# A kernel of Nystrom attention and an MLP: the order of VectorE's work for the coming set of batches, written anew

## The chip, the cores and the metric

The kernel runs on one core of a Trainium2 chip. Its time is the device time of one execution in microseconds (us). Lower is better. Each engine of the core (TensorE, VectorE, ScalarE, GpSimd) works through its own instructions in order, and SyncE issues the DMAs; in the profile they are PE, DVE, ACT, POOL and SP.

## The reference

Eight batches of eight heads, 576 positions, 64 dimensions a head. Softmax attention is approximated over 32 landmarks (means over 18 neighbouring positions), with an iterated pseudo-inverse in between; the result is laid out as 4608 rows of 512 and goes through a layer norm and an MLP with a hidden width of 2048, whose output is added to it.

```python
q_lm = q.reshape(B, H, m, S // m, D).mean(axis=3)      # m = 32 landmarks
k_lm = k.reshape(B, H, m, S // m, D).mean(axis=3)
A, Bm, C = sm(q, k_lm), sm(q_lm, k_lm), sm(q_lm, k)    # sm: softmax of the scaled product
Z = Bm.T / (norm_1(Bm) * norm_inf(Bm) + 1e-06)
for _ in range(6):
    Z = 2 * Z - Z @ Bm @ Z
x = A @ Z @ C @ v                                      # then heads side by side: [8, 576, 512]
xn = (x - mean(x)) / sqrt(var(x) + 1e-06) * g_ln
out = x + maximum(xn @ w_ch1, 0) @ w_ch2
```

## The kernel before

The attention of the batches and the MLP run interleaved on TensorE. Batches 0 and 1 are treated one at a time (`attention`); the others in four **sets**, (2), (3, 4), (5, 6) and (7) (`attention2`). A batch has two **units** of four heads each.

**The MLP stream.** `mlp()` is a generator over nine groups of 512 rows (four **blocks** of 128). Each step gives one matmul: for a group 64 of psh (hidden layer, sixteen tiles of four), with ACT's Relu to hT after each tile, and 64 of pso (output, four tiles of sixteen), with VectorE's ot (scale and add x) after each tile and the store on SP. `fill(n)` takes n steps of it; it returns early when the stream has nothing that it may do. Group 1's input is turned by TensorE (`transposes(1)`: four psxt tiles of four matmuls, each copied to xnT by ACT): during group 0's pso if block 7 is normalized by then, which `ln_ready` tells, and otherwise in a row ahead of group 1's psh. From group 2 on a DMA transpose on SP does it, issued after GpSimd's xn.

**The attention of a set.** `attention2` yields after each of its steps: for each pair of units the scores of k (psb, and psec with ACT's exp ec and VectorE's turn ecT); then the product with v (pscv, gathered for one pair a step) after the gram matrix (psse); six iterations (psn on TensorE, st on VectorE), the first ones with the scores of q for a pair of units (psea, ACT's exp ea); zc (pszc, zcbd); then the **rows**, in pieces of up to 128: two matmuls psy, and on VectorE rcpd and xblk. When a block's rows are complete `block_done` sets off its mean, centering and squares (negm, xn, junk), some of it deferred to `settle` and `a_square`. A set of one batch has 14 steps, a set of two has 21.

**The coming set.** While one set is in its attention the next is prepared (class `Coming`). For each tile of q or k: a load on SP, a cast to fp16 on GpSimd (nat), and on VectorE a **turn** (a transpose, xT<-nat). Each k also has a **sum** over its segments on VectorE (`add_up`: two TENSOR_REDUCE into part); so have the q of the first units, as many as `first_by_pool` says; for the other q GpSimd adds (asum, s) and VectorE turns the result (sT) and adds two halves into part. For each pair of units a **spread** on TensorE (psl<-part) makes the landmarks, copied to lm, from which psb and psec read. These turns, sums and spreads are the **jobs**, in a fixed order; `prepare(c, casts, jobs)` issues so many casts and jobs. Before, one job is issued at every step, and what is left goes into a loop ahead of the set's scores.

**Order.** All engines keep the order in which the program issues (`keep`), stores aside. A matmul that waits for VectorE holds all matmuls behind it. PSUM has three pools: ps1 (one buffer), ps2 (two buffers, taken in turn by psec, pscv, psea, pszc and psy) and psM (three buffers, for psh, pso, psxt and psl).

Batch 1's own attention (generator `a1`) is drained before the sets; its rows come in five pieces, the first one the second half of block 4, the others blocks 5 to 8. Block 7 is the last of group 1.

Of the kernel before, what the change touches and what calls it, by code (L numbers as in the profile page):

```python
# [9 lines left out]
FP16 = mybir.dt.float16  # L10
# [6 lines left out]
P = 128  # L17
# [3 lines left out]
def kernel(  # L21
# [12 lines left out]
    B, H, S, D = q.shape  # L34
# [4 lines left out]
    LM = 32  # L39
# [12 lines left out]
        name=nc.get_next_instruction_name(), act_func_set_id=6, ins=[], outs=[]))  # L52
# [16 lines left out]
    dve, pool, scalar = Ordered(nc.vector), Ordered(nc.gpsimd), Ordered(nc.scalar)  # L69
    act = scalar.activation  # L70

    def MM(o, l, r, rb=0, cb=0, start=True, stop=True, skip=False):
        keep(nc.tensor.matmul(o, l, r, start=start, stop=stop, tile_position=(rb, cb),  # L73
                              skip_group_check=(skip or cb != 0)))
# [88 lines left out]
    for half in range(2):  # L163
        for e in range(2):
            sl = ds(64 * e + 32 * half, 32)
            nc.gpsimd.tensor_copy(
                out=spread16[sl, half, e, :, :],
                in_=ident16[sl, sl][:, None, :].broadcast_to([LM, 2, LM]))
# [23 lines left out]
    for u in range(U):  # L192
        for nm in ("q", "k"):
            cast_qk(0, u, nm, dve)
        if u == 0:

            dve.tensor_copy(out=bones[:], in_=mask4[:, :, None].broadcast_to([P, 4, 32]))
            for i, t in enumerate(zcbd_buf):
                dve.tensor_copy(out=t[:, ds(0 if i % 2 == 0 else 4 * D, 4)],
                                in_=(mask4[:] if i < 2 else heads_of[i % 2]))  # L200
# [43 lines left out]
    asm = ctx.enter_context(tc.tile_pool(name="asm", bufs=2))  # L244
# [263 lines left out]
    class Coming:  # L508
# [38 lines left out]
        def cast(self, i):  # L547
            nm, w = self.parts[i]
            b, u = self.units[w]
            stg = self.stg.pop(i)  # L550
            if nm == "v":
                natv_of[b] = natv_buf[b % NV]
                pool.tensor_copy(
                    out=natv_of[b][:, u, :, :, 0:D].rearrange("p j r d -> p r j d"), in_=stg[:])
                return
            t = nat.tile([P, 2, NJ, D], FP16, name="nat", tag="nat")
            pool.tensor_copy(out=t[:], in_=stg[:])
            self.n16[i] = t
            if nm == "q" and w >= self.first_by_pool:
                s = asum.tile([P, 2, 4, D], FP32, name="asum", tag="asum")  # L560
                s16 = asm.tile([P, 2, D], FP16, name="s16", tag="s16")
                self.sums[i] = s16
                for o, x, y in ((s[:], t[:, :, 0:4, :], t[:, :, 4:8, :]),
                                (s[:, :, 0:2, :], s[:, :, 0:2, :], s[:, :, 2:4, :]),
                                (s[:, :, 0, :], s[:, :, 0, :], s[:, :, 1, :]),
                                (s16[:], s[:, :, 0, :], t[:, :, 8, :])):
                    with nc.allow_low_precision("sums are rounded once, to fp16"):
                        pool.tensor_tensor(out=o, in0=x, in1=y, op=ALU.add)
# [6 lines left out]
        def turn(self, i):  # L575
            nm, w = self.parts[i]
            t = aprep.tile([P, 2, NJ, LM, 2], FP16, name="xT", tag="xT" + nm, bufs=5 if nm == "q" else 4)
            dve.transpose(t[:].rearrange("p r j t x -> p (r j t x)").bitcast(UINT32),
                          self.n16.pop(i)[:].rearrange("p r j d -> p (r j d)").bitcast(UINT32))
            self.xT[nm, w] = t  # L580
            if i in self.sums:
                s = asm.tile([P, 2, LM // 2, 2, 2], FP16, name="sT", tag="sT")
                dve.transpose(s[:].rearrange("p r l a x -> p (r l a x)").bitcast(UINT32),
                              self.sums.pop(i)[:].rearrange("p r d -> p (r d)").bitcast(UINT32))
                dve.tensor_tensor(out=self.part_of(nm, w), in0=s[:, :, :, 0, :], in1=s[:, :, :, 1, :],
                                  op=ALU.add)
# [12 lines left out]
        def spread(self, y):  # L599
            part = self.part.pop(y)  # L600
            psl = psM.tile([P, 2, 8, LM], FP32, name="psl", tag="pm")
            for half in range(2):
                MM(psl[:, half, :, :].rearrange("p k c -> p (k c)"),
                   spread16[:, half, :, :, :].rearrange("p e a w -> p (e a w)"),
                   part[:].rearrange("p n w r l x -> p (n w r l x)"))
            lm = asm.tile([P, 8, 2, LM], FP16, name="lm", tag="lm", bufs=3)
            dve.tensor_copy(out=lm[:].rearrange("p k h c -> p h k c"), in_=psl[:])
            for i, nm in enumerate(("q", "k")):
                for x in range(2):
                    self.lm[nm, 2 * y + x] = lm[:, ds(4 * i + 2 * x, 2), :, :].rearrange(  # L610
                        "p r h (l x) -> p r (h l) x", x=2)
# [126 lines left out]
    def settle():  # L738
        while later:
            later.pop(0)()  # L740
# [156 lines left out]
    def fill(n):  # L897
        for _ in range(n):
            if not next(stream, False):
                return  # L900
# [49 lines left out]
    a1 = attention(1)  # L950
# [6 lines left out]
    cast_v(1)  # L957
    fetch_w2()

    sets = [Coming((2,), 1), Coming((3, 4), 2), Coming((5, 6)), Coming((7,))]  # L960

    def prepare(c, casts, jobs):
        for _ in range(casts):
            if c.casts:
                c.next_cast()
                if not c.loads and c is not sets[-1]:
                    sets[sets.index(c) + 1].next_load()
                else:
                    c.next_load()
        for _ in range(jobs):  # L970
            c.next_job()
# [6 lines left out]
    def a_square():  # L978
        if squares:
            squares.pop(0)()  # L980

    n = 0
    for what in a1:
        fill(fills[what])
        settle()
        if what in ("iteration", "product"):
            a_square()
        if what in ("product", "zc", "rows"):
            n += 1
            prepare(sets[0], 1, 1 if n > 3 else 0)  # L990
    for _ in range(2):
        prepare(sets[0], 1, 1)
        fill(6)

    counts = [[9, 20] + 6 * [6] + [7] + 4 * [7] + [10]]
    counts += [[8, 12, 18, 18, 10, 10, 8, 8, 8, 8, 8] + 10 * [7]]
    counts += [[12, 14, 20, 20, 12, 12, 12, 10, 10, 10, 10] + 10 * [10]]
    counts += [[15, 18] + 6 * [12] + [12] + 5 * [12]]
    for c, after, count in zip(sets, sets[1:] + [None], counts):
        while c.jobs:  # L1000
            prepare(c, 1, 1)
            fill(3)
        for step, _ in enumerate(attention2(c.bs, c)):
            fill(count[step])
            settle()
            if step >= 2:
                a_square()
            if after:
                prepare(after, 1, 1)
    for _ in stream:  # L1010
        pass

# [29 lines left out]
```

## Time and profile before

| | us |
|---|---|
| median of 3 runs | 330.3 (329.87 to 331.22) |
| the profiled execution | 330.62 |
| its span, first to last instruction | 328.9 |
| TensorE busy | 312.6 |
| VectorE busy | 152.3 |
| ScalarE busy | 150.9 |
| GpSimd busy | 121.2 |

The span is shown in forty slices of 8.2 us each, with the busy share in tenths, and the clock that TensorE was granted in tenths of full speed. A row of a timeline has the start, the duration, the engine, line and operation, output and inputs, the shape, how many, and in brackets the idle time ahead and what ended it. A row of a table by groups ends with busy us and the mean in ns, then the idle time ahead. All operations pass through one helper, so they have the same line; their tiles tell them apart.

### The profile page before, as it was taken

What the parts mean: (1) busy time and instruction counts of PE and PEld (TensorE: products, weight loads), DVE (VectorE), ACT (ScalarE), POOL (GpSimd) and SP (SyncE); (2) the same over time, 40 slices, a digit from 0 to 9 for tenths busy, and PEclk for the clock granted to TensorE, in tenths of its full rate; (3) what the DMA queues carried; (4) which work ended last, traced back from release to release, by engine and by line L of the source; (5) the groups of instructions that cost most, each with busy time, mean ns of one, the idle gap of its engine ahead of it and who ended that gap; (6) DMA issues with size and microseconds to landing.
All of it is one profiled execution on the core that took longest, in us unless ns stands there. A gap on an engine that the chain in (4) does not pass through costs nothing.

```text
span 328.9 us, 7899 instructions
## 1 busy us (share of the span) xinstructions
PE 312.6 (95%) x3248; PEld 157.1 (48%) x3248; DVE 152.3 (46%) x398; ACT 150.9 (46%) x295; POOL 121.2 (37%) x186
## 2 busy tenths in 40 slices
PE   8879999599989999989999999999999999999994
PEld 7557654244434444444544444444444444444443
DVE  3677259767987556955464345431243120010012
ACT  3476843339533670469413574563048207305600
POOL 4489877863799290449700020500010300000000
PEclk9999999699999999999999999999999999999999
DMA  7999999948998695871023112320241124032023
GB/s 283 391 387 386 386 389 256 371 125 218 283 272 270 201 258 176 250 140 33 2 66 72 29 32 64 83 48 2 64 103 28 32 64 96 2 75 53 2 56 72
DMA packets 38700, 50.32 MB, mean 153 GB/s; under 512 B 17540, under 2 KB 17800, under 8 KB 38664
## 3 DMA queue, kind: packets, MB, share of 16 engines
q1 hardware_dynamic: 38664, 49.82, 52.7%
q8 instruction: 25, 0.41, 0.6%
q14 instruction: 11, 0.09, 0.1%
HBM read 36.70 MB, written 9.44 MB: 140 GB/s over the span
## 4 chain that ended last, share of the span: by engine, by line
PE 81%; DVE 13%; DMA 3%; issue 1%; SPq 0%; ACT 0%; DVEq 0%
PE psh L73 39%; PE pso L73 31%; DVE xblk L67 3%; DVE part L67 3%; DMA stg<-in_k_dram 2%; PE psn L73 2%; PE psy L73 2%; DVE xT L67 2%; PE pscv L73 2%; DVE ot L67 1%; PE psec L73 1%; DMA xnT<-xn 1%; DVE rcpd L67 1%; PE psea L73 1%; DVE rcv L67 1%
## 5 line engine op out<-in xcount | busy, mean ns | idle before, releaser
L73 PE MATMUL psh<-xnT,w 128*128 128x512 f16 (+1 forms) x640 | 135.1, 358 | 1.2 <-DMA xnT<-xn 1.2
L73 PE MATMUL pso<-w,hT 128*128 128x512 f16 (+1 forms) x592 | 135.0, 377 | 0.6 <-issue 0.6
L67 ACT ACTIVATE hT<-psh 128x512 f16<-128x512 f32 x144 | 84.7, 598 | 89.2 <-PE psh L73 88.9
L73 PEld LDWEIGHTS <-w 128*128 128x128 f16 x640 | 59.1, 98 | 58.9 <-issue 2.9
L73 PEld LDWEIGHTS <-hT 128*128 128x128 f16 x592 | 56.6, 99 | 60.5 <-issue 4.2
L67 DVE SCALAR_TENSOR_TENSOR ot<-pso,rstd,xblk 128x512 f32<-128x512 f32 (+1 forms) x37 | 27.2, 734 | 76.6 <-PE pso L73 76.3
L67 POOL TENSOR_SCALAR negm<-rowsum 128x1 f32<-128x1 f32 x28 | 5.3, 190 | 97.9 <-DVE xblk L67 94.4
L67 ACT ACTIVATE junk<-xblk,negm 128x512 f16<-128x512 f32 x36 | 26.0, 721 | 24.9 <-POOL negm L67 24.8
L67 POOL CAST nat<-stg 128x1152 f16<-128x1152 f32 x28 | 31.8, 1145 | 14.4 <-DMA stg<-in_q_dram 9.4
L67 DVE SCALAR_TENSOR_TENSOR xblk<-psy,rcpd 128x512 f32<-128x512 f32 (+1 forms) x40 | 27.6, 691 | 2.2
L67 DVE SCALAR_TENSOR_TENSOR st<-st,psn 128x128 f16<-128x128 f16 (+2 forms) x36 | 11.4, 316 | 33.3 <-PE psn L73 33.2
L67 POOL CAST natv<-stg 128x1152 f16<-128x1152 f32 x16 | 18.4, 1162 | 7.3 <-DMA stg<-in_v_dram 7.3
L67 DVE TENSOR_REDUCE part<-xT 128x32 f16<-128x576 f16 x30 | 21.0, 743 | 0.0
L67 POOL TENSOR_SCALAR xn<-xblk,negm 128x512 f16<-128x512 f32 x28 | 19.2, 692 | 4.1 <-DMA xnT<-xn 3.1
L67 DVE RECIPROCAL rcpd<-psy 128x8 f32<-128x8 f32 (+1 forms) x40 | 8.1, 202 | 23.9 <-PE psy L73 23.8
L67 DVE STREAM_TRANSPOSE xT<-nat 128x576 uint32<-128x576 uint32 x24 | 18.4, 765 | 0.0
L73 PE MATMUL psy<-zcbd,ea 128*128 128x260 f16 (+1 forms) x80 | 15.7, 276 | 0.9 <-DVE zcbd L67 0.8
L73 PEld LDWEIGHTS <-st 32*32 32x32 f16 x448 | 5.7, 89 | 15.9 <-issue 10.6
L73 PEld LDWEIGHTS <-ea 128*128 128x128 f16 (+1 forms) x80 | 7.3, 100 | 10.5 <-issue 2.2
L67 ACT ACTIVATE ea<-psea 128x576 f16<-128x576 f32 x12 | 7.2, 648 | 10.7 <-PE psea L73 10.7
L67 ACT ACTIVATE ec<-psec 128x576 f16<-128x576 f32 x12 | 8.9, 814 | 6.8 <-PE psec L73 6.8
L67 POOL TENSOR_TENSOR asum<-asum 128x256 f32<-128x256 f32 (+1 forms) x18 | 10.7, 592 | 1.4
(101 smaller groups left out, 209.9 us busy)
## 6 DMA issues: line engine op xcount, KB each, us to landing
stg<-in_q_dram SPq DMA_DIRECT2D x16, 576.0 KB, 7.3
stg<-in_k_dram SPq DMA_DIRECT2D x16, 576.0 KB, 9.0
out_dram<-ot SPq DMA_DIRECT2D x70, 128.0 KB, 2.3
wstg<-in_moe_w_ch_dram SPq DMA_DIRECT2D x16, 512.0 KB, 6.9
stg<-in_v_dram SPq DMA_DIRECT2D x10, 576.0 KB, 7.3
stg<-in_v_dram SPq DMA_DIRECT2D x12, 288.0 KB, 9.2
xnT<-xn SPq DMA_TRANSPOSE x28, 2.5
out_dram<-ot SPq DMA_DIRECT2D x4, 64.0 KB, 2.0
```

What stands on the lines that cost most here:

```text
L67: return lambda *args, **kw: keep(getattr(self.engine, op)(*args, **kw))
L73: keep(nc.tensor.matmul(o, l, r, start=start, stop=stop, tile_position=(rb, cb), skip_group_check=(skip or cb != 0)))
```

## The change

The fill counts and jobs of every step are written out as pairs (count, jobs). For batch 2 both q sums go to GpSimd, for set (3, 4) all but the first. The loop over `a1` ends after the third of its five pieces of rows; the last two follow batch 2's first two steps, each behind that step's matmuls. Set (3, 4) is prepared by one job in eight of batch 2's steps, set (5, 6) by one job in the last seven of the steps of (3, 4), set (7) from the second step of (5, 6) on. The loop ahead of a set's scores gives five matmuls a job and not three. A cast of q or k isn't issued while eight tiles wait for their turn. ACT copies psl to lm, and no longer VectorE. The tiles s16 and sT have four and one buffers, two each before.

```diff
--- before.py
+++ after.py
@@ -558,7 +558,7 @@
             self.n16[i] = t
             if nm == "q" and w >= self.first_by_pool:
                 s = asum.tile([P, 2, 4, D], FP32, name="asum", tag="asum")
-                s16 = asm.tile([P, 2, D], FP16, name="s16", tag="s16")
+                s16 = asm.tile([P, 2, D], FP16, name="s16", tag="s16", bufs=4)
                 self.sums[i] = s16
                 for o, x, y in ((s[:], t[:, :, 0:4, :], t[:, :, 4:8, :]),
                                 (s[:, :, 0:2, :], s[:, :, 0:2, :], s[:, :, 2:4, :]),
@@ -579,7 +579,7 @@
                           self.n16.pop(i)[:].rearrange("p r j d -> p (r j d)").bitcast(UINT32))
             self.xT[nm, w] = t
             if i in self.sums:
-                s = asm.tile([P, 2, LM // 2, 2, 2], FP16, name="sT", tag="sT")
+                s = asm.tile([P, 2, LM // 2, 2, 2], FP16, name="sT", tag="sT", bufs=1)
                 dve.transpose(s[:].rearrange("p r l a x -> p (r l a x)").bitcast(UINT32),
                               self.sums.pop(i)[:].rearrange("p r d -> p (r d)").bitcast(UINT32))
                 dve.tensor_tensor(out=self.part_of(nm, w), in0=s[:, :, :, 0, :], in1=s[:, :, :, 1, :],
@@ -604,7 +604,7 @@
                    spread16[:, half, :, :, :].rearrange("p e a w -> p (e a w)"),
                    part[:].rearrange("p n w r l x -> p (n w r l x)"))
             lm = asm.tile([P, 8, 2, LM], FP16, name="lm", tag="lm", bufs=3)
-            dve.tensor_copy(out=lm[:].rearrange("p k h c -> p h k c"), in_=psl[:])
+            scalar.copy(lm[:].rearrange("p k h c -> p h k c"), psl[:])
             for i, nm in enumerate(("q", "k")):
                 for x in range(2):
                     self.lm[nm, 2 * y + x] = lm[:, ds(4 * i + 2 * x, 2), :, :].rearrange(
@@ -957,11 +957,11 @@
     cast_v(1)
     fetch_w2()
 
-    sets = [Coming((2,), 1), Coming((3, 4), 2), Coming((5, 6)), Coming((7,))]
+    sets = [Coming((2,)), Coming((3, 4), 1), Coming((5, 6)), Coming((7,))]
 
     def prepare(c, casts, jobs):
         for _ in range(casts):
-            if c.casts:
+            if c.casts and (c.parts[c.casts[0]][0] == "v" or len(c.n16) < 8):
                 c.next_cast()
                 if not c.loads and c is not sets[-1]:
                     sets[sets.index(c) + 1].next_load()
@@ -987,26 +987,29 @@
             a_square()
         if what in ("product", "zc", "rows"):
             n += 1
-            prepare(sets[0], 1, 1 if n > 3 else 0)
+            prepare(sets[0], 1, {4: 1, 5: 1, 6: 2}.get(n, 0))
+        if n == 6:
+            break
     for _ in range(2):
         prepare(sets[0], 1, 1)
-        fill(6)
-
-    counts = [[9, 20] + 6 * [6] + [7] + 4 * [7] + [10]]
-    counts += [[8, 12, 18, 18, 10, 10, 8, 8, 8, 8, 8] + 10 * [7]]
-    counts += [[12, 14, 20, 20, 12, 12, 12, 10, 10, 10, 10] + 10 * [10]]
-    counts += [[15, 18] + 6 * [12] + [12] + 5 * [12]]
-    for c, after, count in zip(sets, sets[1:] + [None], counts):
+        fill(8)
+
+    steps = [[(10, 0), (12, 1)] + 6 * [(7, 1)] + [(9, 1)] + 5 * [(6, 0)]]
+    steps += [[(6, 0), (8, 0), (10, 0), (8, 0), (4, 0), (4, 0), (4, 0), (5, 0), (5, 0), (5, 0), (8, 0)]
+              + 3 * [(6, 0)] + 7 * [(7, 1)]]
+    steps += [[(12, 0), (14, 1), (20, 1), (20, 1)] + 6 * [(11, 1)] + [(10, 1)] + 10 * [(10, 1)]]
+    steps += [[(15, 0), (18, 0)] + 6 * [(12, 0)] + [(12, 0)] + 5 * [(12, 0)]]
+    for c, after, plan in zip(sets, sets[1:] + [None], steps):
         while c.jobs:
             prepare(c, 1, 1)
-            fill(3)
-        for step, _ in enumerate(attention2(c.bs, c)):
-            fill(count[step])
+            fill(5)
+        for (count, jobs), _ in zip(plan, attention2(c.bs, c)):
+            fill(count)
             settle()
-            if step >= 2:
-                a_square()
+            a_square()
             if after:
-                prepare(after, 1, 1)
+                prepare(after, 1, jobs)
+            next(a1, None)
     for _ in stream:
         pass
```

## The prediction

> **What bounds the kernel now.** I read first the page's busy shares and slices, then TensorE's timeline for its gaps, then VectorE's timeline at the largest gap, then the table by stretches, last the prices by form. TensorE is busy 95% of the span; from 143 us on it shows no gap. So a change of order can win or lose only by TensorE's gaps before that, and by its clock.
>
> ```profile
> PE 312.6 (95%) x3248; PEld 157.1 (48%) x3248; DVE 152.3 (46%) x398; ACT 150.9 (46%) x295; POOL 121.2 (37%) x186
> PE   8879999599989999989999999999999999999994
> PEclk9999999699999999999999999999999999999999
> ```
>
> The gaps that concern the change, from TensorE's timelines (start, duration; in brackets the idle time ahead and what ended it):
>
> ```profile
> 61.08 0.59 PE L73 MATMUL psl<-part,spread 128*128 128x256 f16 x2 [3.59 <-DVE part L67]
> 96.22 0.39 PE L73 MATMUL psl<-part,spread 128*128 128x256 f16 x2 [1.39 <-DVE part L67]
> ...
> 130.17 0.60 PE L73 MATMUL psy<-zcbd,ea 128*64 128x260 f16 x2 [0.26 <-DVE zcbd L67]
> 136.58 0.38 PE L73 MATMUL psl<-part,spread 128*128 128x256 f16 x2 [0.72 <-DVE part L67]
> 142.91 0.60 PE L73 MATMUL psh<-xnT,w 128*128 128x512 f16 x2 [1.19 <-DMA xnT<-xn]
> ```
>
> Three times a spread (psl) waits for part, the last of VectorE's turns and sums for the next set. VectorE's timeline before the first:
>
> ```profile
> 57.11 0.75 DVE L67 SCALAR_TENSOR_TENSOR ot<-pso,rstd,xblk 128x512 f32<-128x512 f32 x1
> 57.78 0.77 DVE L67 STREAM_TRANSPOSE xT<-nat 128x576 uint32<-128x576 uint32 x1
> 58.58 1.41 DVE L67 TENSOR_REDUCE part<-xT 128x32 f16<-128x576 f16 x2
> 59.91 0.77 DVE L67 STREAM_TRANSPOSE xT<-nat 128x576 uint32<-128x576 uint32 x1
> 60.60 0.20 DVE L67 STREAM_TRANSPOSE sT<-s 128x64 uint32<-128x64 uint32 x1
> 60.84 0.19 DVE L67 TENSOR_TENSOR part<-sT 128x64 f16<-128x64 f16 x1
> ```
>
> It has no idle time there: it is a queue of work that is longer than TensorE's cover. From start to start a turn takes 0.69 us, a sum (two TENSOR_REDUCE) 1.33, an ot 0.67, sT with part 0.46; one piece of rows (rcpd and xblk) 0.85. The stretches around it show what the gap costs beyond itself:
>
> ```profile
> core 0: us, PE busy (x) PEld busy (x) DVE busy (x) ACT busy (x) POOL busy (x), PEclk, DMA share, GB/s
> 53.40:60.20 6.80, 4.10 (x26) 2.04 (x25) 6.66 (x15) 3.16 (x6) 6.08 (x9) 1.00 1.05 333
> 60.20:67.00 6.80, 5.92 (x63) 2.49 (x63) 4.62 (x12) 2.17 (x4) 5.26 (x5) 0.50 1.00 343
> ```
>
> After the 3.59 us of idling the clock is halved for 6.8 us: 5.92 busy us at half speed lose about 3.0.
>
> [...] 3.59 us idle and 0.50 after it; gaps of 1.39 and less left it at 1.00. [...] the spread above waits out the ot and turns ahead of its part. [...] the row hT has 598 ns.
>
> ```profile
> L67 DVE CAST lm<-psl 128x512 f16<-128x512 f32 x6 | 4.1, 684 | 1.0 <-PE psl L73 1.0
> L67 ACT ACTIVATE hT<-psh 128x512 f16<-128x512 f32 x144 | 84.7, 598 | 89.2 <-PE psh L73 88.9
> L67 ACT ACTIVATE ea<-psea 128x576 f16<-128x576 f32 x12 | 7.2, 648 | 10.7 <-PE psea L73 10.7
> L67 ACT COPY xnT<-psxt 128x512 f16<-128x512 f16 x5 | 2.9, 579 | 3.1 <-PE psxt L77 3.1
> ```
>
> **The change, part by part.** An MLP matmul of 512 columns is 0.216 us, a psy pair 0.22.
>
> (1) Two q sums go to GpSimd: VectorE loses 2 x 1.33 and gains 2 x 0.46, GpSimd gains 2 x 2.77 (asum rows 1.156 + 0.730 + 0.455, s 0.426). Six lm copies of 0.684 leave VectorE, and cost ACT about 0.60 each. None ends a wait by itself; they enter below.
>
> (2) Batch 2's spread (61 us before). The third piece of rows starts at 50.02 as before. Then TensorE has 6 + 8 + 8 = 22 pso: ready at 50.24 + 4.75 = 55.0. VectorE's sum of k0 ends, with the third piece, at 53.25 as in the trace; then turn 0.69, sum 1.33, turn 0.69, sT and part 0.46, ot 0.67, turn 0.69, sT and part 0.46: 58.2. GpSimd's second s: the q cast at 48.85, sums from 50.0, cast of q1 from 53.0, sums to 57.1, so it is not last. Idle 3.26 us instead of 3.59: -0.3. The spread is 2.8 us earlier, but two psy pairs, two transposes' groups and six pso no longer lie ahead of it, so the cover has shrunk with the queue. I leave the half clock as it is (the gap is just shorter than before: bounds -3.0 to 0). lm from ACT is ready under five pso: -0.35 (that part of the wait ahead of psb).
>
> (3) The two moved pieces. Block 7 closes group 1 of the MLP, so its four transposes can't be woven into group 0's pso any more: the order has all 16 psxt matmuls in a row behind psea, and psh of group 1 behind them. Block 8's psy takes the PSUM buffer that the second psea tile needs. On VectorE, between the end of the last pso and that buffer's release, stand ot 0.67, the turn of the next set's k0 0.69, and the piece 0.85, with 0.2 of latency 2.4 us; TensorE has psy and psn, 0.35: a new gap of **2.05**. Then ACT has two ea (1.19 in the timeline) and four xnT copies (4 x 0.56) before psh may start: 3.4 us, against 16 transposes of 55 ns, 0.9: a second gap of **2.6**, with latencies. Sum +4.7. [...] I take no second half clock (bounds 0 to +3.4, as 5 us in 6 are idle). GpSimd's negm and xn of block 8 (0.19, 0.69) wait for that xblk, and the casts of the next set's q behind them; their turns come four iterations later, so nothing. Block 8's DMA transpose on SP moves along, needed a group (128 matmuls) later: nothing. Casts and loads stay one for each call of prepare, so SP's loads keep their places to within a few.
>
> (4) Set (3, 4): seven jobs are left for the loop ahead of its scores, with 5 matmuls each. From the last psy to the first spread TensorE has 0.22 + 21 x 0.216 = 4.76; VectorE starts 0.43 after psy (as at 145 us): 0.43 + 0.85 + sum 1.33 + ot 0.66 + turn 0.69 + sum 1.33 = 5.3. Gap 0.6, where 1.39 stood: -0.8.
>
> (5) Set (3, 4)'s own attention has 67 matmuls up to zc, 116 before. Six pso (1.3) under two ec (0.74 each on ACT), four psh (0.86) under two ea: +0.6 for these waits (bounds 0 to 2; the iterations' 0.95 from psn over st to psn is just covered by 1.06).
>
> (6) Set (5, 6)'s jobs now begin at the fourth of ten row pieces, seven matmuls a step, and the rest follow in the loop. From psy 4 to the first spread TensorE has 64 matmuls and 7 psy pairs, 15.4 us. VectorE, from 1.3 us after psy 4: four turns 2.8, four sums 5.3, two turns with sT and part 2.3, six pieces 5.1, four ot 2.6, in all 18.1: 19.4 us. Gap **4.05**, where 0.26 + 0.72 + 1.19 = 2.2 stood (the DMA wait of 142.9 goes, since block 15's rows come 60 matmuls ahead of their group): +1.9. It is longer than 3.59, so a half clock follows: +3.0 (bounds 0 to 3.4).
>
> Sum: -0.3 - 0.35 + 4.7 - 0.8 + 0.6 + 1.9 + 3.0 = +8.75. The profiled execution took 330.6 (span 328.9 and 1.7 around it), so 339.4; the median of three is 0.3 lower: **339.0**.
>
> **Rivals.** (a) The reordering works as VectorE's relief: 1.75 + 4.1 us leave it, the three waits for part and their half clock go, 3.6 + 3.0 + 1.4 + 0.7 + 1.2 = 9.9 less a gap of 2 to 3 at psea: 323. For it: these are the named waits. Against: the work ahead of each spread is shortened, but the matmuls ahead of it too; it decides from where VectorE's queue in (6) is under 15.4 us, 4 less than my sum. (b) The gaps are as summed but more clock is lost: [...] +3.4, and (5) costs its upper bound: 344. For it: 1.4 us of work in 6. [...] (c) Gaps as summed and no half clock at all, with that of 61 us gone too: 339.0 - 6.0 = 333. [...] (d) A wash, 330: only if (3) is hidden, and I see nothing that hides it.
>
> **How the numbers follow.** Half a per cent, 1.6 us, is about what a measurement of this kernel can tell from no change. Forecast 0.64; (b) 0.14; (c) 0.10; (d) 0.04; (a) 0.08. So slower 0.88, same 0.04, faster 0.08. The forecast alone spans 335.5 to 342; the range reaches to (c) and (b): 333 to 345.
>
> **What would show it.** Right: psl of batch 2 near 58.3 with about 3.3 us idle; the second psea tile released by xblk and psh of group 1 by ACT's xnT, two gaps of 2 to 3 us before 78; one gap of about 4 us ahead of set (5, 6)'s first psl and PEclk 0.5 after it; no wait for DMA xnT near it. Wrong: TensorE without a gap over 1 us between psea and psh, or the spread of (5, 6) released by something other than part, or VectorE's queue there idle.

## The result, and the profile after

The changed kernel takes **336.07 us** (median of 4 runs, 334.69 to 336.54), the kernel before 330.61 (4 runs, 329.87 to 331.22). The ratio is 1.016, with a 95% interval of 1.012 to 1.020: slower, by some 5.5 us. The profiled execution of the changed kernel took 336.52 us with a span of 334.8, against 330.62 and 328.9: 5.9 us more to explain. One of the runs reported below, 335.85 us of e1_rows_back, was in a slower state of the chip and is left out.

From the page of the changed kernel, the busy shares and the clock in forty slices (8.4 us each):

```profile
PE 314.9 (94%) x3248; PEld 156.9 (47%) x3248; DVE 147.7 (44%) x392; ACT 155.3 (46%) x301; POOL 126.8 (38%) x194
PEclk9999999787999999999999999999999999999999
```

VectorE did lose 4.6 us of work (152.3 before), ACT gained 4.4 and GpSimd 5.6, as the change says. TensorE's matmuls are the same in number; it is busy 2.3 us longer, most of it by the clock (slices 8 to 10: 10.2 us at half clock in all, 6.8 before), and the rest is gaps. These are its gaps over 0.4 us between 45 and 165 us, from TensorE's timeline of the changed kernel (start, duration, operation; in brackets the idle time ahead and what ended it):

```profile
58.72 0.38 PE L73 MATMUL psl<-part,spread 128*128 128x256 f16 x2 [4.16 <-DVE part L67]
70.01 0.50 PE L73 MATMUL psea<-xT,lm 32*32 32x288 f16 x28 [1.84 <-DVE xblk L67]
72.32 0.38 PE L77 MATMUL psxt<-ident,xn 128*128 128x128 f16 x4 [1.03 <-ACT xnT L67]
73.79 1.44 PE L73 MATMUL psh<-xnT,w 128*128 128x512 f16 x3 [1.09 <-ACT xnT L67]
104.36 0.39 PE L73 MATMUL psl<-part,spread 128*128 128x256 f16 x2 [1.37 <-DVE part L67]
148.16 0.38 PE L73 MATMUL psl<-part,spread 128*128 128x256 f16 x2 [0.47 <-ACT hT L67]
153.87 0.39 PE L73 MATMUL psl<-part,spread 128*128 128x256 f16 x2 [1.90 <-DVE part L67]
```

The reader is to see three things. The first spread still waits for VectorE, longer than before (4.16, not 3.59). Three new gaps, 3.96 us together, stand between 68 and 74 us, where the kernel before had none. And the spreads of the later sets wait 3.74 us in all, 2.11 before, and elsewhere; the wait of 1.19 us for DMA xnT is gone.

The table by stretches of the changed kernel, at the two places where the clock was halved. The second line shown is the stretch just ahead of the second fall:

```profile
core 0: us, PE busy (x) PEld busy (x) DVE busy (x) ACT busy (x) POOL busy (x), PEclk, DMA share, GB/s
59.41:62.83 3.42, 3.42 (x55) 1.19 (x54) 0.86 (x4) 1.31 (x4) 2.51 (x3) 0.50 1.04 371
...
69.65:73.06 3.41, 1.66 (x44) 1.18 (x45) 1.83 (x5) 2.46 (x5) 2.90 (x4) 1.00 0.89 247
73.07:79.89 6.82, 6.10 (x29) 1.83 (x29) 2.04 (x5) 4.21 (x11) 6.42 (x9) 0.50 1.06 219
```

Behind the first gap the half clock is shorter than before (3.4 us, not 6.8); a new one of 6.8 us follows the three new gaps.

To put a number on each stretch, I added up TensorE's lost time: for every matmul the time to the start of the next, less that time as its form has it when undisturbed (the fastest tenth of its form, in whichever of the two traces it is shorter). Gaps and half clock both count in it.

| stretch (its start before and after, us) | lost before | lost after | difference | the prediction's terms |
|---|---|---|---|---|
| start to batch 1's third piece of rows | 16.37 | 15.77 | -0.60 | 0 |
| from there (50.02, 49.42) to group 1's first psh | 8.09 | 12.49 | +4.40 | -0.3 - 0.35 + 4.7 = +4.05 |
| from there (69.94, 73.79) to group 2's first psh | 6.99 | 8.50 | +1.52 | -0.8 + 0.6 = -0.2 |
| from there (106.68, 111.99) to group 3's first pso | 8.83 | 9.27 | +0.44 | +1.9 + 3.0 = +4.9 |
| from there (160.53, 166.29) to the end | 7.94 | 8.08 | +0.15 | 0 |

They add up to the 5.9. The second stretch holds most of the change's price: losses of over 0.6 us at one place go from 3.75 to 8.90 there (the first spread +0.58, the three new gaps 4.57), all smaller ones from 4.34 to 3.59. The second half clock lies in the third stretch and costs 3.3 us there (73.79 to 79.89 us), so the rest of that stretch lost 1.8 us less than before.

### The profile page after: what moved, and what is told of

It reads as the page before. It is cut to its first block, busy times and chain, and to the rows that moved or that the text cites. A ratio compares the mean times of both kernels' runs of the same rounds, so it can differ in the third digit from the quotient of the medians.

```text
span 334.8 us, 7911 instructions
## 1 busy us (share of the span) xinstructions
PE 314.9 (94%) x3248; PEld 156.9 (47%) x3248; DVE 147.7 (44%) x392; ACT 155.3 (46%) x301; POOL 126.8 (38%) x194
## 4 chain that ended last, share of the span: by engine, by line
PE 73%; DMA 9%; DVE 7%; POOL 7%; issue 2%; ACT 1%; SPq 1%; POOLq 0%; DVEq 0%
PE psh L73 33%; PE pso L73 31%; DMA wstg<-in_moe_w_ch_dram 5%; POOL w L67 4%; DMA stg<-in_v_dram 2%; DMA stg<-in_q_dram 2%; DVE part L67 2%; PE psy L73 2%; DVE xT L67 2%; POOL asum L67 1%; DVE ot L67 1%; PE psn L73 1%; PE pscv L73 1%; PE psec L73 1%; DVE xblk L67 1%
## 5 line engine op out<-in xcount | busy, mean ns | idle before, releaser
L73 PE MATMUL psh<-xnT,w 128*128 128x512 f16 (+1 forms) x640 | 138.6, 363 | 1.1 <-ACT xnT L67 1.1
L73 PE MATMUL pso<-w,hT 128*128 128x512 f16 (+1 forms) x592 | 133.1, 376 | 0.0
L67 DVE TENSOR_REDUCE part<-xT 128x32 f16<-128x576 f16 x26 | 18.3, 745 | 0.1
L67 POOL TENSOR_TENSOR asum<-asum 128x256 f32<-128x256 f32 (+1 forms) x22 | 13.0, 593 | 1.7
L67 POOL TENSOR_TENSOR asum<-nat 128x512 f32<-128x512 f16 x11 | 12.7, 1155 | 0.9
```

Of the source, the lines that this page charges most:

```text
L67: return lambda *args, **kw: keep(getattr(self.engine, op)(*args, **kw))
```

## The experiments

My theory: the price is the two moved pieces of rows, some 4 us, and what the edits for VectorE save is small because a spread that comes earlier has less work ahead of it. The rivals: the new counts and jobs of set (3, 4) cost it, or the q sums and copies on GpSimd and ACT do. Later runs ask what would have helped. The table has medians, and ratios to the kernel before on the same chip. Four chips were used (e1 to e4, e5 to e8, e9 to e11, e12); the kernel before took 330.04 to 330.63 us on them.

| run | what it is | us | ratio (95%) |
|---|---|---|---|
| e1_rows_back | changed kernel, rows not moved | 331.83 | 1.0025 (1.0006 to 1.0044) |
| e2_rows_moved | before, rows moved | 334.19 | 1.010 (1.007 to 1.013) |
| e3_old_plan | changed kernel, set (3, 4) with the counts and jobs of before | 340.16 | 1.026 (1.019 to 1.033) |
| e4_relief | before, lm copies on ACT, q sums on GpSimd | 330.02 | 0.996 (0.994 to 0.999) |
| e5_cover | before, 18 more matmuls ahead of the first spread | 336.17 | 1.017 (1.013 to 1.021) |
| e6_cover_cut | e5, 28 fewer matmuls in set (3, 4) | 327.99 | 0.992 (0.989 to 0.996) |
| e7_relief_cover | e4 with cover and cut | 329.36 | 0.996 (0.994 to 0.998) |
| e8_piece_late | changed kernel, block 8's piece a step later | 338.12 | 1.026 (1.022 to 1.029) |
| e9_one_piece | changed kernel, only block 8's piece moved | 334.32 | 1.013 (1.009 to 1.017) |
| e10_best | e6, lm copies on ACT, cover moved | 325.98 | 0.988 (0.985 to 0.990) |
| e11_best_qsum | e10, one q sum more on GpSimd | 322.40 | 0.976 (0.973 to 0.979) |
| e12_tiles_only | e10 with e11's tiles alone | 325.10 | 0.985 (0.979 to 0.990) |

### The rows put back: e1_rows_back

```diff
-        if n == 6:
-            break
...
-            next(a1, None)
```

> The changed kernel, with all five row pieces of batch 1 ahead of the sets again (nothing moved behind batch 2's scores); all else as changed. Theory 1, the move costs the time (two gaps at psea and psh of group 1, and the half clock after them): 329 to 332, no gap between psea and psh, the transposes woven into group 0's pso. Rival, the plan by steps costs it (late jobs, few matmuls in set (3, 4)): 334 to 336. The first spread still waits some 3 us in both.

Measured: 331.83 us (329.85 to 333.42), 4.2 below the changed kernel. None of the gaps at psea and group 1's psh is left. From TensorE's timeline of this run:

```profile
60.95 0.38 PE L73 MATMUL psl<-part,spread 128*128 128x256 f16 x2 [1.34 <-ACT xnT L67]
```

The first spread waits 1.34 us here, and not for part: the two pieces are its cover again. (A psxt at 57.7 us waits 1.16 us, too, for ACT's xnT. At 119 us a psh waited 2.67 us, ended by nothing that the trace shows; other runs have a shorter stall near there or none.) So the move is worth 4.2 of the 5.5 us. Which of the other edits cost the rest, 1.2 us over the kernel before, no run here shows.

### The rows moved alone: e2_rows_moved

```diff
             prepare(sets[0], 1, 1 if n > 3 else 0)
+        if n == 6:
+            break
...
                 prepare(after, 1, 1)
+            next(a1, None)
```

> The kernel before, with the move of the last two row pieces alone (loop over batch 1's attention left after the third piece, one further piece after each of the first two steps). Theory 1: 335 to 338, all 16 transposes behind psea, gaps of about 1.8 and 2.1 us there, half clock after them. Rival (plan): 330 to 332.

Measured: 334.19 us (332.91 to 336.2), a little under what was expected, 3.6 above the kernel before. From its TensorE timeline:

```profile
70.98 0.73 PE L73 MATMUL psea<-xT,lm 32*32 32x288 f16 x28 [2.50 <-DVE xblk L67]
...
74.99 1.01 PE L73 MATMUL psh<-xnT,w 128*128 128x512 f16 x2 [0.89 <-ACT xnT L67]
```

The same two waits with the same releasers come with this edit alone. Moved from either side, the pieces cost 3.6 to 4.2 us: that is shown.

### Set (3, 4) counted as before: e3_old_plan

```diff
-    steps += [[(6, 0), (8, 0), (10, 0), (8, 0), (4, 0), (4, 0), (4, 0), (5, 0), (5, 0), (5, 0), (8, 0)]
-              + 3 * [(6, 0)] + 7 * [(7, 1)]]
+    steps += [[(n, 1) for n in [8, 12, 18, 18, 10, 10, 8, 8, 8, 8, 8] + 10 * [7]]]
```

> The changed kernel, with the counts and the one job a step of before for set (3, 4) alone. Theory 1: 334 to 337, as the gaps at psea and psh stay; the last spread of set (5, 6) then waits under 1 us instead of 1.9. Rival (plan): 330 to 332.

The edit also puts back one job at every step of this set. A miss: 340.16 us (339.24 to 340.7), 4.1 above the changed kernel, where 334 to 337 was expected; the last spread of set (5, 6) has no gap, as expected. One line of its TensorE timeline says why:

```profile
150.09 3.17 PE L73 MATMUL psh<-xnT,w 128*128 128x512 f16 x7 [4.32 <-DMA xnT<-xn]
```

With the old counts the MLP stream is so far ahead that it meets group 3 before block 15's DMA transpose has landed, and the clock is halved with it (148.4 to 155.3 us). So the new counts and jobs of this set are no part of the price; together they save about 4 us in the changed kernel. That rival falls.

### The relief alone: e4_relief

```diff
-            dve.tensor_copy(out=lm[:].rearrange("p k h c -> p h k c"), in_=psl[:])
+            scalar.copy(lm[:].rearrange("p k h c -> p h k c"), psl[:])
...
-    sets = [Coming((2,), 1), Coming((3, 4), 2), Coming((5, 6)), Coming((7,))]
+    sets = [Coming((2,)), Coming((3, 4), 1), Coming((5, 6)), Coming((7,))]
```

with the tiles s16 and sT as in the change.

> The kernel before, with the copies of psl by ACT and the two q sums on GpSimd alone. Relief of VectorE with nothing moved: the first spread waits 0.9 us less, the second 0.5 less: 328.5 to 330. Rival, that a longer GpSimd queue delays the sums or slows VectorE's small operations: 330 to 332.

Measured: 330.02 us (327.74 to 331.36), 0.6 below the kernel before. VectorE's work falls, yet the first spread waits 4.61 us there instead of 3.59, and set (3, 4)'s second one 2.10 instead of 1.39. There are two causes. With a job fewer in the queue, the spread is issued a pass of the loop, and so six matmuls, earlier, and TensorE comes to it 1.1 us earlier. And VectorE ends its queue hardly earlier, since its small additions took longer beside GpSimd's casts. From the whole timeline:

```profile
57.37 2.26 POOL L67 CAST natv<-stg 128x1152 f16<-128x1152 f32 x2
...
58.88 0.79 DVE L67 TENSOR_TENSOR part<-sT 128x64 f16<-128x64 f16 x1
...
60.98 0.39 PE L73 MATMUL psl<-part,spread 128*128 128x256 f16 x2 [4.61 <-DVE part L67]
```

This part took 0.79 us and the next one (60.52 us) 0.41, where the kernel before has 0.19 (60.84 us): 0.82 us of the 0.87 that the moved sum saves. That is the rival that the expectation names. The clock of each run adds to it: the four runs with 0.995 granted took 327.74 to 328.34 us (the kernel before with 0.995 on that chip: 329.37 to 330.50), and ten with 0.984 took 330.02 to 331.36. So at like clock the relief is worth about 2 us, and in ten of nineteen runs a longer half clock takes it back. In the median half a microsecond is left as long as nothing is put ahead of the spread.

### More cover: e5_cover and e6_cover_cut

```diff
     for _ in range(2):
         prepare(sets[0], 1, 1)
-        fill(6)
+        fill(15)
```

and for e6_cover_cut also

```diff
-    counts += [[8, 12, 18, 18, 10, 10, 8, 8, 8, 8, 8] + 10 * [7]]
+    counts += [[8, 10, 12, 12, 8, 8, 6, 6, 6, 6, 6] + 10 * [7]]
```

> The kernel before with 15 instead of 6 stream matmuls behind each of the two jobs ahead of batch 2's scores, 18 matmuls (about 4.2 us at full clock) more cover for the first spread. Theory A (the first gap is VectorE's backlog, worth its 3.6 us and half of the 6.8 us at half clock behind it, and is given back nowhere): first gap under 0.5 us, no half clock behind it, 324 to 326 us. Theory B (the stream only runs ahead: group 3's hidden layer then meets its DMA transpose earlier): first gap gone, the wait for DMA xnT ahead of a psh at about 145 us grows from about 1.2 to 4 to 5 us with a half clock of its own, 329 to 331 us.

> The same with set (3, 4)'s counts cut by 28 stream matmuls, so that the stream meets group 3's input later. Theory A: no different from the run without the cut, 324 to 326 us. Theory B: the wait for DMA xnT is gone and the cover's gain shows, 322 to 326 us, 4 us or more below the run without the cut.

Measured: 336.17 us (333.66 to 336.71) and 327.99 us (325.91 to 329.15), both above the ranges of either theory. The gap at the first spread is gone in both. TensorE's timeline of e5_cover:

```profile
98.46 0.39 PE L73 MATMUL psl<-part,spread 128*128 128x256 f16 x2 [3.79 <-DVE part L67]
...
145.40 2.72 PE L73 MATMUL psh<-xnT,w 128*128 128x512 f16 x6 [4.91 <-DMA xnT<-xn]
```

and of e6_cover_cut:

```profile
140.72 1.46 PE L73 MATMUL psh<-xnT,w 128*128 128x512 f16 x6 [1.60 <-DMA xnT<-xn]
```

Theory B had it, and by more than I gave it: the wait for DMA xnT grew from 1.19 to 4.91 us with 6.8 us of half clock (143.9 to 150.8), and besides 2.4 us of the gap came back at set (3, 4)'s second spread (1.39 to 3.79, with 3.4 us of half clock), which neither theory had. A matmul of the stream that fills one hole is missing in the next. Taken out of set (3, 4)'s steps, it brings the gain: 8.2 us between the two runs. Some of it is another's: a psxt near 60 us waits 1.49 us for ACT's xnT in e5_cover and 0.54 in e6_cover_cut. The wait for DMA xnT is still 1.60 us there, and not gone as expected.

### Relief and cover together: e7_relief_cover

```diff
-    for _ in range(2):
+    for cover in (27, 6):
         prepare(sets[0], 1, 1)
-        fill(6)
+        fill(cover)
...
             prepare(c, 1, 1)
-            fill(3)
+            fill(8)
```

on e4_relief, with e6_cover_cut's counts.

> The kernel before with ACT's copies of psl and the q sums on GpSimd, 27 and 6 stream matmuls behind the two jobs ahead of batch 2's scores, 8 instead of 3 in the loop ahead of the later sets' scores, and the same cut of set (3, 4)'s counts. If cover ahead of the spreads and the relief of VectorE add up: all gaps at a psl under 1 us, 320 to 324 us. If the relief is worth nothing once the spread is covered: the same as the run with cover and cut, 322 to 326 us.

A miss: 329.36 us (327.04 to 330.89), 1.4 above e6_cover_cut. From its whole timeline:

```profile
59.85 0.72 ACT L67 ACTIVATE junk<-xblk,negm 128x512 f16<-128x512 f32 x1 [3.93 <-POOL negm L67]
...
61.19 0.38 PE L77 MATMUL psxt<-ident,xn 128*128 128x128 f16 x4 [2.59 <-ACT xnT L67]
```

GpSimd's second q sum of batch 2 (2.77 us) pushes its casts of v and the negm behind them back; ACT's square of a block (junk) waits for negm, the copy xnT stands behind it in ACT's order, and TensorE's psxt behind that. The second spread of set (3, 4) also still waited 2.66 us: the fill stands behind the last job there, so it covered nothing.

### A step later, and one piece only: e8_piece_late and e9_one_piece

```diff
-        for (count, jobs), _ in zip(plan, attention2(c.bs, c)):
+        for step, ((count, jobs), _) in enumerate(zip(plan, attention2(c.bs, c))):
...
-            next(a1, None)
+            if step != 1:
+                next(a1, None)
```

> The changed kernel with the second of the two moved pieces (block 8's rows) issued after the first iteration's matmuls instead of behind pscv's step. Theory A (psea waits 1.84 us for the PSUM buffer that block 8's psy holds until VectorE's xblk): the wait at psea is gone or under 0.4 us, the two waits of about 1 us for ACT's xnT at block 7's turns and group 1's psh stay, 333 to 335 us. Theory B (the buffer is held longer whenever the piece comes, and the gap only moves one step on): a gap of 1.5 to 2 us at psn or the next psea, 335.5 to 336.5 us.

Measured: 338.12 us (337.77 to 339.58), 2.0 above the changed kernel and outside both ranges. Theory A's mark is there: no gap at psea, and 1.03 and 1.09 us at psxt and psh as before, to the hundredth. So psea's wait was the PSUM buffer under block 8's psy. But the order slid by a step, and further on a wait appeared that the changed kernel doesn't have:

```profile
91.55 0.72 ACT L67 ACTIVATE junk<-xblk,negm 128x512 f16<-128x512 f32 x1 [3.60 <-POOL negm L67]
...
92.90 0.38 PE L73 MATMUL pso<-w,hT 128*128 128x512 f16 x1 [2.56 <-ACT hT L67]
```

It is the chain of e7_relief_cover once more: negm behind GpSimd's asum, s and cast, ACT's Relu behind the square that waits for it. A half clock of 3.4 us follows (93.5 us).

```diff
-        if n == 6:
+        if n == 7:
             break
...
-            next(a1, None)
+            if step == 1:
+                next(a1, None)
```

> The changed kernel with block 7's piece back ahead of batch 2 and only block 8's piece moved, behind the second step's matmuls as before. Theory A (each moved piece has a gap of its own: block 7's the turns in a row ahead of group 1's psh, 2.1 us, block 8's the PSUM buffer that psea waits for, 1.84 us): the turns of group 1 stand between pso matmuls again and their waits for ACT's xnT are under 0.5 us, the wait at psea stays at 1.5 to 2 us, 332.5 to 335 us. Theory B (the two pieces cost together, by the half clock that any gap there sets off): 335.5 to 336.5 us.

Measured: 334.32 us (333.72 to 335.71), in theory A's range, 1.75 below the changed kernel. From TensorE's timeline:

```profile
71.38 0.50 PE L73 MATMUL psea<-xT,lm 32*32 32x288 f16 x28 [0.74 <-DVE xblk L67]
```

The turns stand between pso matmuls again, and no wait is left at group 1's psh. The sizes were missed, though: psea waits 0.74 us and not 1.5 to 2, and a psxt waits 1.53 where under 0.5 was expected, at 57.7 us, for an xnT that stands on ACT behind an xn, which waits 2.45 us for VectorE's negm. Elsewhere the waits changed as well: the first spread's is 2.29 us (4.16 in the changed kernel), that of set (5, 6)'s second one 2.65 (1.90). That each piece has a wait of its own is shown by the two runs; an exact price of each is not.

### A version that beats both: e10_best, e11_best_qsum and e12_tiles_only

On e6_cover_cut:

```diff
-            dve.tensor_copy(out=lm[:].rearrange("p k h c -> p h k c"), in_=psl[:])
+            scalar.copy(lm[:].rearrange("p k h c -> p h k c"), psl[:])
...
     for c, after, count in zip(sets, sets[1:] + [None], counts):
+        if c is sets[1]:
+            fill(10)
...
-    counts += [[8, 10, 12, 12, 8, 8, 6, 6, 6, 6, 6] + 10 * [7]]
+    counts += [[6, 8, 10, 10, 6, 6, 5, 5, 5, 5, 5] + 10 * [7]]
```

> The kernel before with the cover of the run e6_cover_cut, ACT's copies of psl, ten more stream matmuls ahead of the loop before set (3, 4)'s scores, and 17 fewer in the first eleven steps of that set. If the wait of 3.79 us at the first psl of set (3, 4) is VectorE's rows of batch 2 and the wait of 1.60 us for DMA xnT the stream's lead: the first under 1.5 us, the second under 0.5 us, 323 to 326 us. If the cover only moves the waits on: 327 to 329 us, as e6_cover_cut.

e11_best_qsum adds the tiles s16 and sT of the change and one q sum:

```diff
-    sets = [Coming((2,), 1), Coming((3, 4), 2), Coming((5, 6)), Coming((7,))]
+    sets = [Coming((2,), 1), Coming((3, 4), 1), Coming((5, 6)), Coming((7,))]
```

> The run e10_best with set (3, 4)'s second q sum on GpSimd too. If VectorE's 1.33 us less in batch 2's steps shows at that set's first spread: 0.5 to 1.5 us below e10_best. If GpSimd's 2.77 us more holds up its casts or negm: equal or up to 2 us above.

Measured: 325.98 us (325.56 to 327.48) and **322.40 us** (321.38 to 323.88), 2.4% under the kernel before (1.2% without the q sum). As expected of e10_best, set (3, 4)'s second spread (the expectation takes it for the first) waits 0.54 us instead of 3.79, and no wait for DMA xnT is left. The 3.6 us between the two are more than the q sum was expected to bring, and the traces differ before it can act. From the whole timeline of e10_best:

```profile
58.05 1.16 POOL L67 CAST natv<-stg 128x1152 f16<-128x1152 f32 x1 [1.38 <-DMA stg<-in_v_dram]
...
60.75 0.59 PE L77 MATMUL psxt<-ident,xn 128*128 128x128 f16 x4 [1.84 <-ACT xnT L67]
```

and of e11_best_qsum:

```profile
56.77 1.16 POOL L67 CAST natv<-stg 128x1152 f16<-128x1152 f32 x1 [0.51 <-DMA stg<-in_v_dram]
...
59.47 0.38 PE L77 MATMUL psxt<-ident,xn 128*128 128x128 f16 x4 [0.39 <-ACT xnT L67]
```

Up to some 88 us both issue the same instructions on TensorE. A load of v was waited for 1.28 us later in the first, and by GpSimd's negm and ACT's xnT this arrived at TensorE as 1.45 us and a half clock (granted clock 0.993 to 0.995 in every run of e10_best, 0.998 to 1.000 in five of six of e11_best_qsum). The last run has e10_best's instructions in their order, with e11_best_qsum's tiles:

```diff
-                s16 = asm.tile([P, 2, D], FP16, name="s16", tag="s16")
+                s16 = asm.tile([P, 2, D], FP16, name="s16", tag="s16", bufs=4)
...
-                s = asm.tile([P, 2, LM // 2, 2, 2], FP16, name="sT", tag="sT")
+                s = asm.tile([P, 2, LM // 2, 2, 2], FP16, name="sT", tag="sT", bufs=1)
```

> The run e10_best with the four s16 tiles and the one sT tile of e11_best_qsum, but set (3, 4)'s second q sum left on VectorE: the instructions of e10_best in the same order on every engine. Theory A (e11_best_qsum's 3.6 us are the q sum itself): 325.5 to 327 us. Theory B (they are the 1.3 us by which a load of v landed later in e10_best, before the q sum can act, with the wait at psxt and the half clock that follow, and that landing hangs on where the tiles lie): wait at psxt under 0.5 us, 321.5 to 323.5 us.

The median is inconclusive: 325.10 us (323.29 to 327.69), between the two. The wait at psxt is gone, as theory B has it, but the time is not e11_best_qsum's; its profiled execution lost 2.51 us in another stall ended by nothing that the trace shows (a psn at 116.6 us). The clock of each run says more. The three runs with 1.000 granted took 323.29, 324.06 and 324.35 us, and the five of e11_best_qsum with 0.998 to 1.000 took 321.38 to 322.49, 1.9 us less in the mean. The two with 0.993 and 0.995 took 327.06 and 325.86 us, as the six of e10_best do (325.56 to 327.48). So an estimate from these few runs, on two chips, gives the q sum about half of the 3.6 us and the half clock the other half. Whether the later landing belongs to the program or to the execution stays open.

## Why the prediction was right, and where it was wrong

The direction and the main cause were right: step (3), the moved pieces, by the two mechanisms named. The time was 2.9 us lower than forecast, and that it came so near is in part luck, for two errors stood against each other: step (6) hardly happened, 4.5 us less in its stretch, and a second half clock, which the sum had at nothing, cost 3.3 us.

**Step (3) held.** From the whole timeline of the changed kernel, the queue ahead of psea and of psh:

```profile
67.69 0.75 DVE L67 SCALAR_TENSOR_TENSOR ot<-pso,rstd,xblk 128x512 f32<-128x512 f32 x1 [0.22 <-PE pso L73]
...
69.26 0.69 DVE L67 SCALAR_TENSOR_TENSOR xblk<-psy,rcpd 128x512 f32<-128x512 f32 x1
...
70.60 1.19 ACT L67 ACTIVATE ea<-psea 128x576 f16<-128x576 f32 x2 [3.07 <-PE psea L73]
...
71.68 2.06 ACT L67 COPY xnT<-psxt 128x512 f16<-128x512 f16 x4
```

VectorE does an ot and the coming set's turn before block 8's xblk lets the buffer go: 1.84 us, 2.05 predicted. ACT then does two ea and four xnT before psh: two gaps of 1.03 and 1.09, one of 2.6 predicted; four transposes ran between them, since a copy frees a psM buffer. What failed in this step is its last term: "I take no second half clock". It came, 6.8 us long, as rival (b) had it. That gaps of 2 to 3 us leave the clock whole was my estimate, which no trace showed, and the trace of the kernel before already speaks against it: the gap ahead of its first spread began at 57.49 us, and the clock fell at 60.18, 2.7 us into it, with TensorE busy for 0.73 of the 3.41 us before. Its length varies from run to run: two of the changed kernel's four runs had a granted clock of 0.985 as the profiled one and took 336.5 us, the other two 0.989 and 0.990 and took 335.62 and 334.69.

**Step (2), the first spread: mis-sized.** Predicted at 58.3 with 3.26 us idle, measured 58.72 with 4.16. Everything up to it ran 0.6 us early (piece 3 at 49.42), VectorE's queue as well, so that is not what widened the gap. The last piece was not the 0.46 us of sT and part. GpSimd's s was the last after all by 0.31 us, and then:

```profile
57.47 2.27 POOL L67 CAST natv<-stg 128x1152 f16<-128x1152 f32 x2
...
57.84 0.83 DVE L67 TENSOR_TENSOR part<-sT 128x64 f16<-128x64 f16 x1
```

part took 0.83 us instead of 0.19, and ended about as the first of the two casts beside it did (57.84 + 0.83 = 58.67; half of the two casts is over at 58.61). I had priced part from its row at 60.84 us of the kernel before, where the first of two casts had 0.04 us left. The wait and the 0.64 us more of part make up the 0.9 us by which the gap was too small.

**Step (2)'s half clock** was left at 6.8 us and was 3.4 us, a gain of some 1.7 us, within the bounds. What the traces show is where the gap lay: before, it reached 0.9 us beyond the fall at 60.18, and the half clock lasted 6.83 us; after, it ended 0.7 us ahead of the fall at 59.41, and the half clock lasted 3.41. That the one made the other is my estimate, from the busy shares in the last section. The change did not aim at that, so this is luck too.

**Steps (4) and (5)**: set (3, 4)'s first spread had no gap (0.6 predicted), since it does not wait for the sums and the turn of the second pair that the prediction counted, as in step (6). The 1.39 us set against it was the second spread's: in the kernel before, the first one (91.20 us) had no gap either. The second spread waits 1.37 us after the change, so nothing was gained there. As a sum the stretch was to bring -0.2, and brought +1.52 with 3.3 of the second half clock in it; the compression of (5) doesn't show as a gap over 0.4 us.

**Step (6) failed.** A gap of 4.05 us ahead of set (5, 6)'s first psl and a half clock, +4.9 together, against a measured +0.44. The matmuls' side was right (psy 4 at 131.94, the spread at 148.16). VectorE's queue was too long: I counted four turns and four sums for k. The first spread reads only the parts of the first pair of units, two turns and two sums fewer, 2 x (0.69 + 1.33) = 4.04, just the gap that I predicted. VectorE's timeline of the changed kernel:

```profile
145.19 0.20 DVE L67 TENSOR_TENSOR part<-sT 128x64 f16<-128x64 f16 x1
```

Its parts were ready at 145.4, 2.8 us ahead; the spread waited 0.47 us for a Relu, which is a sign of being wrong that the prediction named ("the spread of (5, 6) released by something other than part"). The rest of the queue falls on the second spread, behind 15 more psh matmuls, as 1.90 us, and the clock stayed full. That the DMA wait of 142.9 goes was right.

**The rivals.** (a), relief, fell: e4_relief gives 0.6 us. (b)'s half clock came, and its total didn't, since step (6) was missing. (c), 333, is as far below the measured time as the forecast is above it, and its premise fell: both half clocks are there.

## What to carry to other kernels

Work that is moved behind a wait takes its cover with it: ask what stood ahead of the waiting instruction because of it, which buffer it holds where it goes, and what can no longer be woven in. An engine's relief pays only with something to run ahead of its consumer, and that filler is missing later: e5_cover lost 5.7 us with it, e6_cover_cut gained 2.5 when it was taken from where the stream was too early, and e11_best_qsum 7.6 us, in part by its clock, when each wait got its share. Work that goes to a neighbouring engine can come back as a slower small operation (part took 0.83 us beside GpSimd's cast, 0.19 in the kernel before): look at what runs beside it. When a wait for a queue is costed, count only what its reader reads.

## What the runs showed of the hardware

- Between two changes TensorE's clock held its value for 54.61, 6.83 and 262.83 us in the kernel before, and for 54.61, 3.41, 10.24, 6.83 and 256.00 us in the changed kernel: whole multiples of 3.41 us in both traces. In steps of 3.41 us laid from such a change, TensorE was busy for 0.73 us of the step ahead of the fall at 60.18 in the kernel before, and for 0.69 and 1.66 us of those ahead of the falls at 59.41 and 73.06 in the changed kernel, the last of them broken by three short gaps; after a step with 1.51 us (151.57 to 154.98) the clock did not fall.
- Counted by such steps in the fourteen traces, the clock fell to half 22 times before the last matmul, each time after a step in which TensorE was busy for 0 to 49%. All 20 steps with 41% or less were followed by a fall, two of the five with 44 to 49%, and none with 53% or more. The half clock held after the seven steps with 52 to 83% busy and ended after those with 88 to 100%, so it came in pieces of 3.4, 6.8 and, in e2_rows_moved, 10.2 us. These are counts of this kernel's traces; what sets the clock, they do not show.
- Where the first fall came against the first gap differed: at 60.18 us in the kernel before, 2.7 us into it, and at 59.41 us in the changed kernel, 0.7 us behind its end.
- TensorE stood still for 2.67 us (e1_rows_back) and 2.51 us (e12_tiles_only) with nothing in the trace that ended it.
- The addition into part on VectorE took 0.19 to 0.22 us in 79 of its 141 instances in the fourteen traces, and 0.24 to 1.21 us in the other 62. Each of these 62 ended 0.03 to 0.05 us after an instruction of GpSimd had ended (a cast, an addition of asum or s, or xn). The longest is in e3_old_plan, at 126.40 us, beside a cast from 126.41 to 127.58.
